# Linear attention beside a gated feed-forward block: Q projected token-wise next to K, denominators on VectorE, phi(q) turned by the DMA crossbar

## The chip, the cores and the metric

One core of one Trainium2 chip. The metric is device microseconds of one execution. Kernels sent together ran on the same chip, each beside runs of the kernel before. Traces count from the start of the span, which is 1.7 to 1.9 us shorter than the time of the same execution.

## The reference, cut to what matters

```python
xn = _layernorm(x)                               # x: 1 x 2048 x 576, bf16
q, k, v = split(xn @ wqkv)                       # 32 heads of 18
phi = lambda t: where(t > 0, t + 1, exp(t)) + 1e-6
kv  = einsum("bhsd,bhse->bhde", phi(k), v)
z   = einsum("bhsd->bhd", phi(k))
num = einsum("bhqd,bhde->bhqe", phi(q), kv)
den = einsum("bhqd,bhd->bhq", phi(q), z)[..., None] + 1e-6
A   = (num / den) @ wo
B   = (gelu(x_ @ w_gate) * (x_ @ w_up)) @ w_down # x_ = xn, 576 -> 4608 -> 576
out = x + A + B
```

The feed-forward block is most of the work. Attention has no softmax: it needs phi(k) for all tokens, then small 18x18 products per head, then one denominator per token and head.

## The kernel before: the parts that the change and the argument touch

The program runs a projection stage (16 tiles of 128 tokens), then four blocks of 512 tokens, each of them 18 gate/up steps and then a down projection. A number after "block", as in "block 3", means one such step of two units; "the second block" means the second 512 tokens. G is the product of xn and phi(k), summed over the tokens; with V's weights it gives kv. m is kv times wo, and the "m stage" builds it inside the first down projection. K comes out token-wise (tokens on partitions), Q channel-wise (channels on partitions), in five chunks of up to 126 channels; so phi(q) is at once in the layout that the final product wants.

```python
def k_half(n, hf):                               # token-wise: xnT is the stationary operand
    for kt in range(KT):
        nc.tensor.matmul(ps_all[:, k_bank(n, hf), :HALF], lhsT=xnT[:, kt, n*P:(n+1)*P],
                         rhs=wqkv_sb[:, kt, D + hf*HALF : D + (hf+1)*HALF], ...)

def q_unit(i):                                   # channel-wise: the weights are stationary
    for kt in range(KT):
        nc.tensor.matmul(ps, lhsT=wqkv_sb[:, kt, q0:q0+rows], rhs=xnT[:, kt, sc*SC:(sc+1)*SC], ...)

# phi before: relu and exp on ScalarE, (eps on GpSimd), max and add on VectorE

def den_mm(sc, c, bank):                         # denominators on TensorE, 512 tokens at once
    nc.tensor.matmul(ps, lhsT=zrep[:rows, c, :rows], rhs=pqT[:rows, c, sc*SC:(sc+1)*SC], ...)
    den_evac(sc, c, ps)                          # VectorE: PSUM -> SBUF, + eps

def den_norm(sc, c, q, pieces):
    for h in range(0, w, P):
        nc.vector.reciprocal(out=d[:, h:h+P], in_=d[:, h:h+P])
    # ... GpSimd then multiplies pqT by d

def gu_pair(sc, k):                              # one gate/up step
    for i in range(GUB):                         # GUB = 2 units, each on two PSUM banks
        if blk > 0:
            load_gu(blk + NWBUF - 1, i)          # weights three steps ahead, SyncE's queue
        u.p1()
    # ... load one slice of the down weights in steps 2 to 13 of the first block
    for i, (b, u) in enumerate(units):
        u.p2()
        nc.scalar.activation(out=gl[:], in_=ps_all[:, b[0], :], func=ACT.Gelu_apprx_tanh)
        nc.vector.tensor_tensor(out=hT[...], in0=ps_all[:, b[1], :], in1=gl[:], op=ALU.mult)

def m_stage(c, acc_bank):                        # inside the first down tile, every six matmuls
    for hf in range(2):
        b = (acc_bank + 2 + (2*c + hf) % 6) % 8
        nc.tensor.matmul(ps_all[:rows, b, :HALF], lhsT=kvT[...], rhs=wo2[...], ...)
```

## Time and profile before

| | before |
|---|---|
| time, median of the first 3 runs | 524.57 us |
| span of the trace | 521.7 us |
| TensorE busy | 99% |
| first projection matmul | 7.41 us |
| first gate/up starts, ends | 71.59, 142.93 us |
| period of the second and third block | 111.45, 111.46 us |

Read it as a chain of stages, each at TensorE's pace: the projection stage to 71.59 us, then four times gate/up (70.04 us of matmuls, 71.34 in the first block with the paired denominators) and down (40.2 us in the last block, 41.4 where denominator matmuls are hooked in). After the first 13 us TensorE hardly waits at all. So a change can help only by taking matmul time away, or by starting TensorE sooner. The prediction shows the lines behind this.

### The profile page before, as it was taken

What the parts mean: (1) busy time and instruction counts of PE and PEld (TensorE: products, weight loads), DVE (VectorE), ACT (ScalarE), POOL (GpSimd) and SP (SyncE); (2) the same over time, 40 slices, a digit from 0 to 9 for tenths busy, and PEclk for the clock granted to TensorE, in tenths of its full rate; (3) what the DMA queues carried; (4) which work ended last, traced back from release to release, by engine and by line L of the source; (5) the groups of instructions that cost most, each with busy time, mean ns of one, the idle gap of its engine ahead of it and who ended that gap; (6) DMA issues with size and microseconds to landing.
All of it is one profiled execution on the core that took longest, in us unless ns stands there. A gap on an engine that the chain in (4) does not pass through costs nothing.

```text
span 521.7 us, 10641 instructions
## 1 busy us (share of the span) xinstructions
PE 516.1 (99%) x4498; PEld 313.5 (60%) x4498; DVE 250.9 (48%) x436; ACT 143.1 (27%) x293; POOL 35.2 (7%) x55
## 2 busy tenths in 40 slices
PE   7999999999999999999999999999999999999997
PEld 6777755555587754444577744444777544445775
DVE  7996565876358323433388133333584233433101
ACT  6898442332320013323200032232000123322000
POOL 2021000211001100000012000000011000000000
PEclk9999999999999999999999999999999999999999
DMA  8334609899500045555300155555100355440000
GB/s 279 62 64 118 154 25 264 254 269 266 157 12 13 13 124 155 144 156 160 93 13 13 41 166 145 155 156 155 29 23 13 103 161 158 140 134 2 13 11 24
DMA packets 106282, 57.89 MB, mean 111 GB/s; under 512 B 13370, under 2 KB 105722, under 8 KB 106234
## 3 DMA queue, kind: packets, MB, share of 16 engines
q1 hardware_dynamic: 105626, 56.55, 38.8%
q8 instruction: 35, 0.57, 0.5%
q10 hardware_dynamic: 608, 0.66, 0.4%
q14 instruction: 13, 0.11, 0.1%
HBM read 52.86 MB, written 2.36 MB: 106 GB/s over the span
## 4 chain that ended last, share of the span: by engine, by line
PE 97%; DMA 1%; ACT 1%; DVE 0%; issue 0%
PE ps_all L313 55%; PE ps_all L677 27%; PE ps_all L289 4%; PE ps_all L682 4%; PE ps_all L245 3%; PE ps_all L342 3%; DMA wqkv_sb<-in_A_wqkv_dram 1%; PE ps_all L451 1%; PE ps_all L433 0%; PE ps_all L659 0%; ACT xnT L234 0%; ACT L114 0%; ACT phi_e L265 0%; ACT phi_e L269 0%; DVE hT L273 0%; DVE res L685 0%
## 5 line engine op out<-in xcount | busy, mean ns | idle before, releaser
L313 PE MATMUL ps_all<-xnT,wg 64*128 64x512 bf16 x1152 | 272.6, 376 | 0.0
L313 PE MATMUL ps_all<-xnT,wu 64*128 64x512 bf16 x1152 | 271.8, 376 | 0.0
L648 DVE TENSOR_TENSOR hT<-ps_all,gl 128x512 bf16<-128x512 f32 x144 | 99.5, 691 | 161.9 <-ACT gl L647 161.2
L647 ACT ACTIVATE gl<-ps_all 128x512 f32<-128x512 f32 x144 | 86.1, 598 | 314.3 <-PE ps_all L313 297.4
L313 PEld LDWEIGHTS <-wu 64*128 64x128 bf16 x1152 | 108.3, 94 | 66.3
L313 PEld LDWEIGHTS <-wg 64*128 64x128 bf16 x1152 | 108.3, 94 | 66.1
L677 PE MATMUL ps_all<-wd_sb,hT 128*128 128x288 bf16 x1152 | 147.0, 286 | 0.0
L677 PEld LDWEIGHTS <-hT 128*128 128x128 bf16 x1152 | 112.3, 98 | 30.6 <-issue 1.3
L475 DVE RECIPROCAL den_sb<-den_sb 126x128 f32<-126x128 f32 (+1 forms) x80 | 68.3, 911 | 0.5
L685 DVE TENSOR_TENSOR res<-ps_all,x_sb 128x288 bf16<-128x288 f32 x32 | 14.7, 458 | 88.0 <-PE ps_all L682 88.0
L313 PE MATMUL ps_all<-xnT,wr 64*128 64x512 bf16 x288 | 55.1, 376 | 0.0
L478 POOL TENSOR_TENSOR pqT<-pqT,den_sb 126x512 bf16<-126x512 bf16 (+3 forms) x25 | 24.2, 966 | 317.3 <-DVE den_sb L475 279.4
L682 PE MATMUL ps_all<-m_sb,pqT 126*128 126x288 bf16 (+1 forms) x160 | 24.9, 285 | 0.0
L313 PEld LDWEIGHTS <-wr 64*128 64x128 bf16 x288 | 14.4, 94 | 16.9 <-issue 0.7
L245 PE MATMUL ps_all<-wqkv_sb,xnT 128*128 128x288 bf16 x160 | 22.5, 286 | 0.9 <-DMA wqkv_sb<-in_A_wqkv_dram 0.8
L289 PE MATMUL ps_all<-hT,xn 128*128 128x288 bf16 (+4 forms) x176 | 22.4, 275 | 0.0
L289 PEld LDWEIGHTS <-xn 128*128 128x128 bf16 (+1 forms) x176 | 17.5, 102 | 4.1
L245 PEld LDWEIGHTS <-xnT 128*128 128x128 bf16 x160 | 15.4, 98 | 6.9 <-issue 1.4
L682 PEld LDWEIGHTS <-pqT 126*128 126x128 bf16 (+1 forms) x160 | 15.5, 97 | 4.1
L342 PE MATMUL ps_all<-xnT,wqkv_sb 128*126 128x512 bf16 (+1 forms) x70 | 17.4, 378 | 0.0
L273 DVE SCALAR_TENSOR_TENSOR hT<-ps_all,phi_e 128x288 bf16<-128x288 f32 x32 | 13.2, 450 | 4.6 <-ACT phi_e L269 4.0
L265 ACT ACTIVATE phi_e<-ps_all 128x288 f32<-128x288 f32 x32 | 12.9, 410 | 3.6 <-PE ps_all L245 2.1
(68 smaller groups left out, 173.8 us busy)
## 6 DMA issues: line engine op xcount, KB each, us to landing
wg<-in_B_w_gate_dram SPq DMA_DIRECT2D x72, 256.0 KB, 2.9
wu<-in_B_w_up_dram SPq DMA_DIRECT2D x72, 256.0 KB, 3.5
wd_sb<-in_B_w_down_dram SPq DMA_DIRECT2D x12, 432.0 KB, 4.6
wr<-in_B_w_gate_dram SPq DMA_DIRECT2D x72, 32.0 KB, 2.7
wr<-in_B_w_up_dram SPq DMA_DIRECT2D x72, 32.0 KB, 3.1
out_dram<-res SPq DMA_DIRECT2D x15, 144.0 KB, 1.8
x_sb<-in_A_x_dram SPq DMA_DIRECT2D x3, 576.0 KB, 7.1
wqkv_sb<-in_A_wqkv_dram SPq DMA_DIRECT2D x2, 576.0 KB, 4.7
```

The costliest lines, as they stand in the source:

```text
L245: nc.tensor.matmul(ps_all[:, k_bank(n, hf), :HALF], lhsT=xnT[:, kt, n * P:(n + 1) * P], rhs=wqkv_sb[:, kt, D + hf * HALF:D + (hf + 1) * HALF],
L273: nc.vector.scalar_tensor_tensor(out=out_, in0=ps, scalar=0.0, in1=e, op0=ALU.max, op1=ALU.add)
L289: nc.tensor.matmul(ps_all[:m, b, col:col + w], lhsT=xn[:, n, j0:j0 + m], rhs=pk[:, n, d0:d0 + w], start=(n == 0 and col == 0), stop=(n == ...
L313: return nc.tensor.matmul(self.outs[i], lhsT=self.lhs(i, rows, kt), rhs=self.rhs(i, rows, kt), start=start, stop=stop, skip_group_check=True,)
L342: nc.tensor.matmul(ps, lhsT=wqkv_sb[:, kt, q0:q0 + rows], rhs=xnT[:, kt, sc * SC:(sc + 1) * SC], start=(kt == 0), stop=(kt == KT - 1),)
L475: nc.vector.reciprocal(out=d[:, h:h + P], in_=d[:, h:h + P])
L478: nc.gpsimd.tensor_tensor(out=pqT[:rows, c, cols], in0=pqT[:rows, c, cols], in1=d, op=ALU.mult)
L647: nc.scalar.activation(out=gl[:], in_=ps_all[:, b[0], :], func=ACT.Gelu_apprx_tanh)
L648: nc.vector.tensor_tensor(out=hT[:, GUB * k + i, :], in0=ps_all[:, b[1], :], in1=gl[:], op=ALU.mult)
L677: nc.tensor.matmul(acc, lhsT=hT[:, f, j * P:(j + 1) * P], rhs=wd_sb[:, f, hs], start=(f == 0), stop=False,)
L682: nc.tensor.matmul(acc, lhsT=pqT[:rows, c, ts_], rhs=m_sb[:rows, c, hs], start=False, stop=(c == NCH - 1),)
L685: nc.vector.tensor_tensor(out=res[:, hs], in0=acc, in1=x_sb[:, n, hs], op=ALU.add)
```

## The change

Its intent: with a row of ones in the transposed tokens, the projection gives t + 1, so phi is max(min(exp(t), 1), t + 1): one exp and one VectorE pass. Q is projected like K, token by token. The denominators are then sums along the free axis, on VectorE, and TensorE does not have to do them; the scaled phi(q) has to be turned into the channel layout, by DMA crossbar transposes. The norm of tiles 3 to 15 goes to GpSimd. Cut to its core:

```diff
-    banks = _Ring([6, 7, 0, 1, 2, 3, 4, 5])
+    banks = _Ring([4, 5, 6, 7, 2, 3, 0, 1])
+    KQ_BANK = (6, 4)                                  # indexed by which: 0 is Q, 1 is K
+    def kq_mm(n, which, hf):                          # Q and K alike, 288 columns each
+        c = which * D + hf * HALF
+        for kt in range(KT):
+            nc.tensor.matmul(ps_all[:, KQ_BANK[which] + hf, :HALF], lhsT=xnT[:, kt, n*P:(n+1)*P],
+                             rhs=wqkv_sb[:, kt, c:c + HALF], ...)
+    def kq_exp(n, which, hf):
+        nc.scalar.activation(out=e[:], in_=ps_all[...], func=ACT.Exp, bias=neg1[:], scale=1.0)
+    def kq_phi(n, which, hf):
+        nc.vector.scalar_tensor_tensor(out=(pq, pk)[which][...], in0=e[:], scalar=1.0,
+                                       in1=ps_all[...], op0=ALU.min, op1=ALU.max)
 ... (q_unit, q_pair, q_relu, q_exp, q_eps, q_sum, den_mm, den_pair, den_evac, den_norm go)
     def ln_norm(n, c0=0, c1=D):
-        nc.vector.tensor_scalar(
+        (nc.vector if n < TD else nc.gpsimd).tensor_scalar(
 ...
+    def den_mul(n):    # VectorE: (pq + eps) * z, 576 columns
+    def den_inv(n):    # VectorE: reduce over 18, + eps, reciprocal of 32
+    def den_scale(n):  # VectorE: (pq + eps) * 1/den, two pieces
+    def den_transpose(n):
+        nc.sync.dma_start_transpose(pqT[:, :, n*P:(n+1)*P], den_pn[n][:])
 ... (a small planner now orders the projection stage from durations and landing times)
+    W_AT = {1: 5.60, 0: 7.90}                         # when K's and Q's weights are thought to land
+    den_jobs = [(job, n) for n in range(NS) for job in (den_mul, den_inv, den_scale, den_transpose)]
 ... in gu_pair, after each unit's eviction:
+            if den_jobs and blk > 0:
+                job, n = den_jobs.pop(0)
+                job(n)
```

K's weights are now asked for third on the one queue, ahead of the third x load, and Q's fifth; before, K's went on ScalarE's queue.

## The prediction

> **What bounds the kernel now.** I read the first page top down, then the chain of waits, then the chain in order of time, then the timeline at three places: the start, one projection period, the turn into the first down projection. The busy table and the chain come first.
>
> ```profile
> PE 516.1 (99%) x4498; PEld 313.5 (60%) x4498; DVE 250.9 (48%) x436; ACT 143.1 (27%) x293; POOL 35.2 (7%) x55
> ...
> PE 97%; DMA 1%; ACT 1%; DVE 0%; issue 0%
> PE ps_all L313 55%; PE ps_all L677 27%; PE ps_all L289 4%; PE ps_all L682 4%; PE ps_all L245 3%; PE ps_all L342 3%; DMA wqkv_sb<-in_A_wqkv_dram 1%; PE ps_all L451 1%; PE ps_all L433 0%; PE ps_all L659 0%; ACT xnT L234 0%; ACT L114 0%; ACT phi_e L265 0%; ACT phi_e L269 0%; DVE hT L273 0%; DVE res L685 0%
> ...
> L475 DVE RECIPROCAL den_sb<-den_sb 126x128 f32<-126x128 f32 (+1 forms) x80 | 68.3, 911 | 0.5
> ```
>
> 97% of the chain is TensorE, and gate/up (L313) and down (L677) are 82% of it; the change touches neither's own matmuls. The 68.3 us of reciprocals on VectorE never appear in the chain, so by themselves they are worth nothing. Busy TensorE is not TensorE at its limit, so I checked the spacing, in the chain in order of time (start, length, what):
>
> ```profile
> 65.78 77.21 PE ps_all L313 x714
> ...
> 185.48 70.04 PE ps_all L313 x648
> ...
> 260.86 4.41 PE ps_all L677 x36
> 266.11 4.41 PE ps_all L677 x36
> ...
> 508.70 4.41 PE ps_all L677 x36
> 513.73 4.41 PE ps_all L677 x36
> ```
>
> 648 half-array matmuls in 70.04 us are 108.1 ns each; those of the second token block, where there is nothing else, come gap-free. 714 x 108.1 = 77.2 us: the first block's line holds also the 54 of the paired Q units and 12 of the paired denominators, without a gap. In the down part the period is 513.73 - 508.70 = 5.03 us at the end and 266.11 - 260.86 = 5.25 where a denominator matmul is hooked in. So what is saved is matmul time that is removed, plus idle TensorE at the start. One projection period (timeline, TensorE):
>
> ```profile
> 26.79 0.91 PE L289 MATMUL ps_all<-hT,xn 128*128 128x288 bf16 x7
> 27.54 1.24 PE L342 MATMUL ps_all<-xnT,wqkv_sb 128*126 128x512 bf16 x5
> 28.62 1.39 PE L245 MATMUL ps_all<-wqkv_sb,xnT 128*128 128x288 bf16 x10
> 29.85 0.91 PE L289 MATMUL ps_all<-hT,xn 128*128 128x288 bf16 x7
> ```
>
> From start to start: seven G matmuls 0.75 us, five Q matmuls of 512 columns 1.08, ten K matmuls of 288 columns 1.23. The start, and the turn into the first down part:
>
> ```profile
> 7.41 0.77 PE L245 MATMUL ps_all<-wqkv_sb,xnT 128*128 128x288 bf16 x5 [0.79 <-DMA wqkv_sb<-in_A_wqkv_dram]
> ```
>
> ```profile
> 142.80 0.69 DVE L648 TENSOR_TENSOR hT<-ps_all,gl 128x512 bf16<-128x512 f32 x1 [2.33 <-ACT gl L647]
> ...
> 143.66 0.69 DVE L648 TENSOR_TENSOR hT<-ps_all,gl 128x512 bf16<-128x512 f32 x1 [0.17 <-ACT gl L647]
> ...
> 143.84 0.26 PEld L659 LDWEIGHTS <-kvT 126*126 126x126 bf16 x2
> ```
>
> The first K matmul starts at 7.41 because its weights land then; the copy of the transposed tokens had ended at 6.65 + 0.24 = 6.89, by the same view. At the turn, VectorE is done with the last gate/up bank at 144.35.
>
> **What the Trainium skill says.** "TensorE: Matmul & The Clock Gate", Back-to-back issue gap: a warm matmul of N columns costs N/2.4 + 2.5 ns. That is 215.8 for 512 and 122.5 for 288; the trace has 1.08/5 = 216 and 1.23/10 = 123. It agrees, and TensorE is warm. "VectorE: DVE Perf Modes", The TRN2 errata: an fp32 tensor_tensor takes (N+151)/0.96 ns; 512 gives 691, the trace's 691. I use it for the new VectorE passes. Its perf-mode tier table puts tensor_reduce at 1x, which no trace here shows yet. "GPSIMD Engine Reference", Engine selection: a one-input pass is roughly at line rate; the trace's 126x512 pass took 620 ns. "DMA: Bandwidth & Descriptors", Rules for kernel authors: a transpose next to ordinary DMAs needs no serializing. The before trace has its 12 transposes away from the heavy traffic (2.6 us to landing, 1.2 us of the issuing queue each), so it cannot confirm that.
>
> **The change part by part.**
>
> *Q projection.* Removed: 14 whole units x 5 x 0.216 = 15.1 us and 54 half-array matmuls x 0.108 = 5.8, together 20.9. Added: 16 tiles x 10 matmuls of 288 columns = 16 x 1.225 = 19.6. Saves 1.3 us.
>
> *Denominators off TensorE.* 12 half-array matmuls in the first gate/up: 12 x 0.108 = 1.3 us. 14 full ones hooked into the first three down parts: 14 x 0.216 = 3.0. Saves 4.3, all on the path.
>
> *Start.* K's weights go third on one queue, behind two x tiles (288 KB) in place of four. The windows table moved 171 GB/s in 0-5 us and 347 in 5-10, so 288 + 648 KB are through at about 5.2 us (estimate). The limit then is tile 0's transposition, and its last column block no longer waits for a GpSimd copy: about 6.8 where it was 7.41. One PE transposition fewer saves 0.3. Between 7.41 and 12.65 TensorE idled about 0.6 us; I keep 0.5.
>
> *A new wait after the last Q tile.* The third part of G now takes banks 4 and 5, the Q banks. Its first matmul needs exp (0.41) and phi (0.46) of the last Q half to be through, about 1.0 us after that half's last matmul. TensorE has 0.45 us of work meanwhile for the first bank and 0.1 for the second: idle 0.55 + 0.5 = 1.05 us. Before, Q and G never met there.
>
> *Sum of the projection stage.* 32 projections x 1.225 = 39.2, G 16 x 0.75 = 12.0, the rest of G 8.0, kv and z 1.75, transposes 0.6: 61.6. From 6.8, + 0.5 + 1.05: gate/up starts at 70.0, before at 65.78 + 54 x 0.108 = 71.6. Gain 1.6 us.
>
> *VectorE in that stage.* Per tile two stats 0.82, one aggregate 0.21, four phi 1.82: 2.85 us against a TensorE period of 2.45 + 0.75 = 3.2. The norm goes to GpSimd, 576/512 x 620 = 0.7 us (estimate). ScalarE: 0.49 + 4 x 0.41 = 2.1. All fit, VectorE with only 11% to spare.
>
> *VectorE in gate/up.* Gone: 68.3 (reciprocals) + 13.4 (evictions). New per tile, estimates by the page's formula: multiply 0.76, reduce 0.76 + small add and reciprocal 0.5, scale 0.68 + 0.23: 2.9 us over four units. With four eviction passes of 0.69 that is 5.7 of 4 x 1.945 = 7.8 us. It fits; nothing on the path.
>
> *The first down part.* The bank order became 4,5,6,7,2,3,0,1. The stage that builds m uses, six matmuls in, banks 0 and 1, which are now those of the last gate/up unit (before they were used at twelve). A den multiply (0.76) stands in VectorE's order between the last two evictions, so the last ends at 143.49 + 0.76 + 0.69 = 144.94 on the old clock, where that matmul was due at 143.96. Loss 1.0 us, once.
>
> *DMA.* 16 transposes of 160 KB in gate/up, eight of them in the first block, where the DMA engines are 86-107% busy from 80 to 130 us. Each costs about 0.9 us of the 16 engines (share 0.28 over 5 us with 1.6 transposes in 20-25 us). That delays loads by some 5 us at most by the end; gate weights are asked for three blocks (11.7 us) ahead and took up to 5.8 us to land. I expect no stall.
>
> Total: -1.6 - 1.3 - 3.0 + 1.0 = -4.9 us. 524.57 - 4.9 = 519.7.
>
> **The rivals.**
> 1. *VectorE becomes the bound of the projection stage.* For it: 89% load in a fixed order, with GpSimd beside it. Against: before, it was at 4.5-4.8 of 5 us busy in 15-40 us and TensorE never idled. If a tile took 3.4 in place of 3.2, it costs 3 us: 522.5 to 523.
> 2. *The transposes starve gate/up.* For: full DMA engines, and the queue that issues the weights now waits for VectorE's scale and then issues a transpose for 1.2 us. Against: the 11.7 us of lead, and that even the slowest weight load needed half of that. If it happened, 2 to 6 us in the first block: 522 to 526.
> 3. *The two bubbles are not there and the start is clean.* If VectorE and ScalarE are quicker than I order them, the whole 2 us stay: 517.5.
> 4. *Freeing VectorE and GpSimd speeds up gate/up.* Against: 108.1 ns a matmul is the issue gap itself. Nothing is to be had.
>
> **Range and chances.** Removed matmul time (5.6 us) is firm. The start is good to 1 us, each bubble to 1. That gives 517.0 to 522.4. Faster than 2% needs 10.5 us, twice what is removed, and no stall exists that could be added to it: 3%. Slower by 2% would take a stall of 15 us against the plan: 3%. Within 2%: 94%.
>
> **What would show it.** First real matmul at 6.8; a stage period of 3.2; gate/up from about 70.0; the first gate/up in 70.0 us and not 71.3; 5.03 us per half tile in all down parts after the first; about 1 us idle at the first G matmul on bank 4 and 5, released by VectorE's phi, and 1 us at the second m matmul pair, released by VectorE's hT. I am wrong if TensorE idles inside the projection stage on phi, or in gate/up on a weight DMA, or if gate/up's matmuls no longer come every 108 ns.

## The result, and the profile after

The changed kernel takes 519.90 us (median of 4, 519.53 to 520.3) beside 524.24 for the kernel before (4 runs). Ratio 0.9924, 95% interval 0.991 to 0.9938: 0.8% faster, inside 2%. A ratio here isn't quite the ratio of the medians (0.9917). So the gain is 4.0 us by the ratio and 4.3 by the medians, where 4.9 was predicted.

Stage by stage, from the traces (the end of the first gate/up is the start of the first matmul of the m stage):

| | before | changed | gain |
|---|---|---|---|
| first projection matmul | 7.41 | 7.11 | |
| first gate/up starts | 71.59 | 70.49 | 1.10 |
| length of first gate/up | 71.34 | 70.51 | 0.83 |
| from there to the second gate/up | 42.55 | 42.41 | 0.14 |
| second block | 111.45 | 110.37 | 1.08 |
| third block | 111.46 | 110.36 | 1.10 |
| fourth block to the end of the span | 113.31 | 113.66 | -0.35 |
| span | 521.7 | 517.8 | 3.9 |

The last row isn't TensorE's: from the fourth block's start to the start of the last group of matmuls are 109.6 us in both traces, and what follows that group takes 0.3 us longer in the changed one.

The page of the changed kernel, for the lines that answer to those of before:

```profile
PE 510.4 (99%) x4497; PEld 314.2 (61%) x4497; DVE 202.0 (39%) x407; ACT 133.5 (26%) x260; POOL 36.0 (7%) x32
...
PE 94%; DMA 3%; SPq 1%; ACT 1%; DVE 0%; POOL 0%; issue 0%
...
L213 POOL TENSOR_SCALAR xn<-x_sb,mv,rstd 128x576 bf16<-128x576 bf16 x13 | 29.6, 2287 | 8.7 <-ACT rstd L210 8.7
```

VectorE gave up 49 us of busy time, and the kernel gained 4. TensorE is still the chain, but 94% of it in place of 97%: DMA and its issuing queue (SPq) have come into it. The third line is one that the prediction had wrong by a factor of three: a norm on GpSimd takes 2287 ns.

The chain in order of time (start, length, what) says where those DMAs sit:

```profile
3.41 5.96 DMA wqkv_sb<-in_A_wqkv_dram
...
15.76 2.30 POOL xn L213
18.08 3.53 DMA xnT<-xn
...
23.80 2.45 PE ps_all L243 x20
26.25 0.74 PE ps_all L274 x7
...
60.20 8.74 PE ps_all L274 x71
...
127.66 5.42 DMA wr<-in_B_w_up_dram
133.13 7.09 PE ps_all L298 x63
...
183.41 70.04 PE ps_all L298 x648
```

There are three new waits: for Q's weights at the start, for the slow norm and transpose of an early tile, and for a small gate/up weight load near 133 us. The steady projection period is 2.45 + 0.74 = 3.20 us as planned (L243 is Q and K, L274 is G). And 71 G matmuls run in 8.74 us right after the last Q tile, without a gap: the bubble that I had predicted there isn't there. The two waits at TensorE, from its timeline, then the one at the turn into the first down projection:

```profile
7.11 1.39 PE L243 MATMUL ps_all<-wqkv_sb,xnT 128*128 128x288 bf16 x10
9.41 2.00 PE L243 MATMUL ps_all<-wqkv_sb,xnT 128*128 128x288 bf16 x15 [0.91 <-DMA wqkv_sb<-in_A_wqkv_dram]
```

```profile
141.48 0.75 DVE L358 SCALAR_TENSOR_TENSOR den_t<-pq,zb 128x576 f32<-128x576 bf16 x1
...
142.15 0.68 DVE L564 TENSOR_TENSOR hT<-ps_all,gl 128x512 bf16<-128x512 f32 x1
...
142.88 0.28 PE L574 MATMUL ps_all<-wo,kvT 126*126 126x288 bf16 x1 [0.56 <-DVE hT L564]
```

The den multiply stands between the last two evictions, and the second m matmul pair waits for the bank that the last eviction reads: it was due 0.12 us after 142.03 and came at 142.88, 0.73 us late.

### The profile page after: what moved, and what is told of

Same layout as the page of the kernel before. It is cut to its first block, busy times and chain, and to the rows that moved or that the text cites. A ratio compares the mean times of both kernels' runs of the same rounds, so it can differ in the third digit from the quotient of the medians. Undisturbed runs are those within 1.5% of the kernel's fastest.

```text
span 517.8 us, 10582 instructions
## 1 busy us (share of the span) xinstructions
PE 510.4 (99%) x4497; PEld 314.2 (61%) x4497; DVE 202.0 (39%) x407; ACT 133.5 (26%) x260; POOL 36.0 (7%) x32
## 4 chain that ended last, share of the span: by engine, by line
PE 94%; DMA 3%; SPq 1%; ACT 1%; DVE 0%; POOL 0%; issue 0%
PE ps_all L298 53%; PE ps_all L592 27%; PE ps_all L243 6%; PE ps_all L597 4%; PE ps_all L274 4%; DMA wqkv_sb<-in_A_wqkv_dram 1%; DMA wr<-in_B_w_up_dram 1%; DMA xnT<-xn 1%; POOL xn L213 0%; SPq L93 0%; PE ps_all L345 0%; DVE hT L564 0%; PE ps_all L574 0%; ACT phi_e L250 0%; DVE den_t L358 0%
## 5 line engine op out<-in xcount | busy, mean ns | idle before, releaser
L298 PE MATMUL ps_all<-xnT,wr 64*128 64x512 bf16 x288 | 56.2, 376 | 0.1
L243 PE MATMUL ps_all<-wqkv_sb,xnT 128*128 128x288 bf16 x320 | 42.5, 286 | 1.3 <-DMA wqkv_sb<-in_A_wqkv_dram 0.9
L243 PEld LDWEIGHTS <-xnT 128*128 128x128 bf16 x320 | 30.4, 98 | 9.0 <-issue 1.1
L250 ACT ACTIVATE phi_e<-ps_all,neg 128x288 f32<-128x288 f32 x64 | 31.6, 499 | 15.1 <-PE ps_all L243 11.4
L213 POOL TENSOR_SCALAR xn<-x_sb,mv,rstd 128x576 bf16<-128x576 bf16 x13 | 29.6, 2287 | 8.7 <-ACT rstd L210 8.7
L274 PE MATMUL ps_all<-hT,xn 128*128 128x288 bf16 (+4 forms) x176 | 22.6, 275 | 0.3 <-ACT xnT L232 0.3
L274 PEld LDWEIGHTS <-xn 128*128 128x128 bf16 (+1 forms) x176 | 17.6, 101 | 4.4 <-issue 0.5
L255 DVE SCALAR_TENSOR_TENSOR pq<-phi_e,ps_all 128x288 bf16<-128x288 f32 x32 | 14.5, 452 | 10.1 <-ACT phi_e L250 9.8
L255 DVE SCALAR_TENSOR_TENSOR hT<-phi_e,ps_all 128x288 bf16<-128x288 f32 x32 | 14.4, 453 | 3.4 <-ACT phi_e L250 3.0
L202 DVE BATCH_NORM_STATS2 stats<-x_sb 128x6 f32<-128x288 bf16 x32 | 13.0, 441 | 2.1 <-DMA x_sb<-in_A_x_dram 2.1
```

The costliest lines, as they stand in the source:

```text
L202: nc.vector.bn_stats(out=ln_raw[n][:, h, :], in_=x_sb[:, n, h * HALF:(h + 1) * HALF])
L213: (nc.vector if n < TD else nc.gpsimd).tensor_scalar(out=xn[:, n, c0:c1], in0=x_sb[:, n, c0:c1], scalar1=mv[:, n, 0:1], scalar2=rstd[:, n: ...
L243: nc.tensor.matmul(ps_all[:, KQ_BANK[which] + hf, :HALF], lhsT=xnT[:, kt, n * P:(n + 1) * P], rhs=wqkv_sb[:, kt, c:c + HALF], start=(kt == ...
L250: nc.scalar.activation(out=e[:], in_=ps_all[:, KQ_BANK[which] + hf, :HALF], func=ACT.Exp, bias=neg1[:], scale=1.0,)
L255: nc.vector.scalar_tensor_tensor(out=(pq, pk)[which][:, n, hf * HALF:(hf + 1) * HALF], in0=e_tiles[n, which, hf][:], scalar=1.0, in1=ps_al ...
L274: nc.tensor.matmul(ps_all[:m, b, col:col + w], lhsT=xn[:, n, j0:j0 + m], rhs=pk[:, n, d0:d0 + w], start=(n == 0 and col == 0), stop=(n == ...
```

## The experiments

My theory after this: the gain is the removed matmul time, about 5.6 us, and the rest of the account is waits at the edges. The rivals: VectorE's relief has a share in the gain; and each wait has another cause than the one that I name. Twelve kernels ran, on three chips, each beside the kernel before. The traces' main numbers first, side by side. The waits are the idle time that the profile gives, counted from the modelled end of the matmul before; from start to start they are about 0.17 us longer. "Late" is by how much the loads that block 13 issues (three steps ahead, so for block 16) were asked for after TensorE had begun block 13 (its start is gate/up's start + 13 x 3.891 us). Block 16, due at 132.75 us in the changed kernel, is where TensorE waited near 133.

| | time | ratio | wait for Q's weights | gate/up starts | first gate/up | late |
|---|---|---|---|---|---|---|
| changed | 519.90 | 0.9924 | 0.9 | 70.49 | 70.51 | 4.8 |
| changed again (control) | 520.50 | 0.9932 | 1.6 | 71.20 | 70.91 | 5.4 |
| Q on banks 4, 5 | 521.92 | 0.9965 | 1.6 | 72.34 | 70.98 | 5.3 |
| other ring | 519.67 | 0.9921 | 1.5, and 0.3 for K's | 71.53 | 70.95 | 5.3 |
| four tiles only | 519.96 | 0.9924 | 1.3 | 70.91 | 70.69 | 3.4 |
| plan's constants | 519.47 | 0.9916 | none | 70.19 | 70.48 | 5.0 |
| transposes from ScalarE | 521.22 | 0.9959 | 0.6 | 70.87 | 71.61 | 4.2 |
| all norms on VectorE | 518.91 | 0.9913 | 1.5 | 70.40 | 70.04 | 4.1 |
| paced down weights | 519.91 | 0.9920 | 1.0 | 70.89 | 70.03 | 2.8 |
| transposes behind loads | 520.10 | 0.9927 | 1.5 | 71.39 | 70.03 | 2.6 |
| combined | 518.01 | 0.9879 | none | 68.43 | 70.04 | 0.4 |

### What pays: VectorE time or TensorE time? (b_norecip, b_den128)

Both are the kernel before with one thing less; both give a wrong result.

```diff
-        for h in range(0, w, P):
-            nc.vector.reciprocal(out=d[:, h:h + P], in_=d[:, h:h + P])
```

> The kernel before with its 80 reciprocals on VectorE left out (68.3 us of VectorE's time; the result is wrong on purpose). Theory: VectorE's denominator work lay beside TensorE's and was worth nothing; the time stays at 524.2, within 0.3 us, and TensorE's placement does not move. Rival: the reciprocals held evictions and so TensorE, and freeing VectorE is part of what the change gained: 1 us or more less.

Measured: 523.37 us beside 523.65, ratio 1.0003 (0.999 to 1.0015). 68 us less VectorE work moved nothing. The theory holds.

```diff
-        nc.tensor.matmul(ps, ..., rhs=pqT[:rows, c, sc * SC:(sc + 1) * SC], ...)
+        nc.tensor.matmul(ps[:, 0:P], ..., rhs=pqT[:rows, c, sc * SC:sc * SC + P], ...)
```

> The kernel before with the 14 denominator matmuls of 512 columns in the down projections cut to 128 columns (the result is wrong on purpose; VectorE's and GpSimd's work stay as they are). Theory: removed TensorE time is paid in full: 14 x (216 - 56) ns = 2.2 us less, 522.0. Rival: a matmul hooked in this way costs its wait or its eviction and not its columns; then the time stays near 524.2.

Measured: 521.59 us, ratio 0.9966 (0.9953 to 0.9978), 0.34% of 523.65 or 1.8 us less. The chain in order of time of the run without reciprocals, then of the run with short denominator matmuls:

```profile
185.40 70.03 PE ps_all L313 x648
296.86 70.04 PE ps_all L313 x648
```

```profile
185.00 70.04 PE ps_all L313 x648
295.66 70.04 PE ps_all L313 x648
```

The period from one gate/up to the next is 111.46 in the first and 110.66 in the second: 0.80 us for five matmuls shortened by 160 ns each. The denominator matmuls are paid one for one, and the reciprocals' VectorE time not at all.

### The bubble after the last Q tile (a_qbanks)

```diff
-    KQ_BANK = (6, 4)
+    KQ_BANK = (4, 6)
```

> The changed kernel with Q's and K's PSUM banks exchanged, so that the third part of G does start on the banks that the last Q tile leaves. My theory is that the 1.05 us bubble that I predicted after the last Q tile is real physics, and was missing only because I had read the bank table the wrong way round (Q is on 6 and 7, K on 4 and 5). It expects TensorE to idle about 1.0 us at the first two G matmuls after the last Q tile, released by phi on VectorE, and the time to rise by 1.0 us over the changed kernel's 519.9, to 520.9. The rival, that exp and phi are quick enough to be hidden by themselves, expects no idle there and 519.9.

Timeline of TensorE in this run:

```profile
59.55 1.39 PE L243 MATMUL ps_all<-wqkv_sb,xnT 128*128 128x288 bf16 x10
61.40 0.28 PE L274 MATMUL ps_all<-hT,xn 128*128 128x288 bf16 x1 [0.47 <-DVE pq L255]
62.01 8.78 PE L274 MATMUL ps_all<-hT,xn 128*128 128x289 bf16 x70 [0.33 <-DVE pq L255]
```

Ten projection matmuls take 1.22 us, so the first G matmul was due at 60.77 and came 0.63 us late; the second was due 0.12 us after the first and came 0.49 us late. (The brackets count from the modelled end of the matmul before, and so show less.) The bubble is real when the banks meet: 1.12 us, released by phi of Q, where I had said 0.55 + 0.5. From the start of these ten to gate/up are 12.79 us here and 11.67 in the changed kernel, the same 1.12. So the mechanism and its size were right and the premise wrong: I had taken the bank table to be (K, Q) where it is indexed (Q, K). The time rose from 0.9924 to 0.9965, 0.41% or 2.1 us, more than the bubble; the trace also has 0.7 us more wait for Q's weights than the changed kernel's first one, and 0.5 us more in the first gate/up. Together these are 2.3 us, which is the difference of the two spans (520.1 and 517.8). The last two vary from run to run, as the control shows.

### The same kernel again (a_same)

No edit.

> The changed kernel once more, not altered, as the control of this call. In the traces so far the same code waited 0.6 to 1.8 us for the Q weights at the start and 0.8 to 3 us on a weight DMA in the first gate/up block. Theory: these two waits are of the DMA engines' timing and vary from execution to execution, so this trace shows 0.6 to 1.8 us for the first and 0.3 to 2 for the second, and the time is 0.9924 of before within 0.0013. Rival: they are fixed by the code, and this trace repeats 0.91 and 0.8.

Measured: 520.50 us (519.58 to 521.38), ratio 0.9932 (0.9919 to 0.9945). The wait for Q's weights was 1.6 us where it had been 0.91, and the first gate/up 70.91 us where it had been 70.51. The code is the same. Both waits are on DMA, and both vary by more than most of the effects looked for below. So small edits are judged by the piece of the trace that they touch, and times only where the intervals allow it. What makes the landing vary isn't known from these runs.

### The wait at the turn into down (a_ring, a_den4)

```diff
-    banks = _Ring([4, 5, 6, 7, 2, 3, 0, 1])
+    banks = _Ring([4, 5, 6, 7, 0, 1, 2, 3])
```

> The changed kernel with the PSUM ring in the order 4,5,6,7,0,1,2,3, so that the last gate/up unit of a block leaves banks 2 and 3, which the stage that builds m asks for twelve matmuls into the first down projection in place of six. Theory: the 0.73 us that TensorE lost in that stage waiting for VectorE's last eviction was the bank order's doing; it goes, and the time falls by 0.7 us to about 519.2. Rival: VectorE's den multiply in front of the eviction holds the matmul whatever the bank, and the idle time stays or moves to another matmul: 519.9.

Timeline of this run at the turn:

```profile
142.97 0.75 DVE L358 SCALAR_TENSOR_TENSOR den_t<-pq,zb 128x576 f32<-128x576 bf16 x1
143.52 0.41 PE L574 MATMUL ps_all<-wo,kvT 126*126 126x288 bf16 x2
143.63 0.68 DVE L564 TENSOR_TENSOR hT<-ps_all,gl 128x512 bf16<-128x512 f32 x1
```

The two matmuls of the second pair run as one group while the last eviction is only beginning, with the den multiply still in its place: with this bank order there is no wait. From the end of the first gate/up to the second are 41.68 us in place of 42.41, so the 0.73 us is gained in full there. The time, 0.9921, shows no gain over 0.9924; this trace waited 1.8 us for the projection weights (1.5 of it for Q's) and its first gate/up took 70.95 us. On time the run is inconclusive; on the mechanism it isn't.

```diff
-            if den_jobs and blk > 0:
+            if den_jobs and blk > 0 and (sc > 0 or den_jobs[0][1] < TPC):
```

> The changed kernel with the denominator jobs of only the four tiles that the first down projection needs done in the first gate/up block (four crossbar transposes there in place of eight, none while the down weights stream in the second half), the others later. Theory: the transposes are what delays the gate/up weights; the wait of about 0.5 us on the small weight DMA near 133 us goes, the first gate/up block takes 70.05 us from first to last matmul, and with no den multiply before the last eviction the 0.73 us wait of the m stage goes too: 1.2 us less, 518.7. Rival: the weights are late because of the down weights alone; then only the 0.7 us go and the wait on the weight DMA stays: 519.2.

Measured: 519.96 us, ratio 0.9924, no gain: a miss. With no den multiply between the last evictions the second m pair came 0.33 us late (143.08, due at 142.75) in place of 0.73: the ring alone costs a third of a microsecond, the den multiply the rest. The weight wait did not go. It moved from 133 to 118 us, and the first gate/up took 70.69 us. So the loads can run late with four transposes, all in the first half (one trace); neither my theory (it goes) nor the rival (it stays at 133, with the down weights alone to blame) describes that.

### What delays the gate/up weights? (a_actq, a_pace, a_defer)

The issuing queue of the changed kernel, around block 3, which TensorE begins at 70.49 + 3 x 3.89 = 82.2 us:

```profile
80.65 0.59 SPq L530 DMA_DIRECT2D wd_sb<-in_B_w_down_dram  x1
83.64 1.24 SPq L385 DMA_TRANSPOSE pqT<-pn  x1
85.39 0.39 SPq L162 DMA_DIRECT2D wg<-in_B_w_gate_dram  x1
```

The queue stands from 81.2 to 83.6 us, until VectorE has scaled the tile; then it issues the transpose; then the load that block 3 issues for block 6, 3.2 us late. I had written that this lead was 11.7 us and safe.

```diff
-        nc.sync.dma_start_transpose(pqT[...], den_pn[n][:])
+        nc.scalar.dma_start_transpose(pqT[...], den_pn[n][:])
```

> The changed kernel with the 16 crossbar transposes of phi(q) issued from ScalarE's queue in place of the queue that issues the weights. It tells two ways apart in which the transposes could delay the gate/up weights. If it is the issuing queue (1.2 us of issue for each transpose, and the wait for VectorE's scale in front of it), the wait of about 0.5 us on the weight DMA near 133 us goes, and the time falls by 0.5 us or, if ScalarE's evictions are now held by the issue, rises by up to 1 us with idle in gate/up on PSUM. If it is the DMA engines' bandwidth, the wait on the weight DMA stays: 519.9.

Measured: 521.22 us, ratio 0.9959. SyncE's queue was relieved (43.7 us of issue in the first gate/up in place of 58.2), and yet the first gate/up grew to 71.61 us: 1.6 us over its 70.04. The small weight loads took up to 7.0 us to land (median 5.6) in place of 6.3 (4.3). ScalarE was held as well: before the gelu at 135.72 us it stood for 5.2 us, a transpose's issue among them, and the second m pair came 1.21 us late in place of 0.73. In gate/up itself TensorE's waits are on a small weight load (0.2 and 0.8 us). So the run mixes the ways that it was to tell apart, and the time rose by more than the 1 us that I had allowed. It does show that relieving this queue isn't enough: with the transposes on a second queue the weights land later. Why is open. The DMA engines' share was 1.12 to 1.22 from 80 us on, but 0.98 to 1.32 in the changed kernel, so it doesn't tell the two apart; and in the second block these transposes took 4.9 us to land (median) in place of 2.6.

```diff
-        elif sc == 0 and k >= 2:
+        elif sc == 0 and k >= 2 and k % 4 != 1:
             load_wd_slice()
```

> The changed kernel with the twelve slices of down weights spread over blocks 2 to 16 in place of 2 to 13 (every fourth block asks for none); nothing else moves. Theory: in 80 to 130 us the DMA engines are asked for 576 + 432 KB of weights and 80 KB of transposes per 3.89 us block, more than they move (259 to 287 GB/s), so the loads fall behind; at 576 + 324 + 80 KB they keep up, the wait on the weight DMA near 133 us goes, and the first gate/up block takes 70.1 us in place of 70.5: 0.5 us less. Rival: the lateness comes from the transpose's place in the issuing queue and stays.

```diff
+        while turned:                              # after the step's weight loads
+            den_transpose(turned.pop(0))
-    ... for job in (den_mul, den_inv, den_scale, den_transpose)]
+    ... for job in (den_mul, den_inv, den_scale, turned.append)]
```

> The changed kernel with each crossbar transpose moved behind the next block's weight loads in the issuing queue, so that the loads no longer stand behind a wait for VectorE's scale. Theory of the order: block 3's weights were asked for at 85.39, 3.2 us after TensorE had begun that block, and that lateness is the lead that is missing near 133; with it restored to under 1 us at block 3 the wait on the weight DMA goes, 0.5 us less. Rival, the engines' bandwidth: the loads are asked for earlier but land no earlier, and a wait of about 0.5 us or more stays.

The chain in order of time of the run with paced down weights, then of the run with transposes behind the loads:

```profile
70.95 69.19 PE ps_all L298 x640
```

```profile
71.45 69.19 PE ps_all L298 x640
```

Both took the wait away altogether: 640 matmuls in one piece, where the changed kernel's chain breaks near 133 us; the first gate/up is 70.03 us in each, and no weight DMA is left among TensorE's waits. I had set them up as rivals and they aren't. The loads run out of lead, and relief at either place is enough. That they start late behind a transpose is shown by the queue; that the engines are asked for more than they move is not shown, since pacing also takes issues out of the same queue, and a block's 1088 KB (of 1024 bytes) in 3.89 us would be 286 GB/s (estimate), where the windows table has 223 to 287 GB/s moved between 80 and 130 us. Each result rests on one trace. The "late" column goes with it: at 4.1 us late or less with the transposes on SyncE's queue TensorE didn't wait, at 4.8 or more it did, the four-tile run excepted, whose wait fell in an earlier block. In time neither is clear of the control: 0.9920 (0.9908 to 0.9932) and 0.9927 (0.9915 to 0.9938) against 0.9932.

### The order at the start (a_plan)

```diff
-    W_AT = {1: 5.60, 0: 7.90}
+    W_AT = {1: 6.80, 0: 9.40}
-            step(("norm", n), "POOL", 0.80, ...
+            step(("norm", n), "POOL", 2.29, ...
-                step(("exp", n, which, h), "ACT", 0.45, ...
+                step(("exp", n, which, h), "ACT", 0.50, ...
```

> The changed kernel with three constants of its ordering plan set to what its own trace shows: Q's weights land at 9.4 us (planned 7.9), a GpSimd norm takes 2.29 us (planned 0.80), an exp 0.50 (planned 0.45). Only the order of the instructions changes. Theory: TensorE's 0.91 us wait for the Q weights and the waits of 0.3 us for the late tiles come from a plan that puts Q of tile 0 too early; with K of tile 1 ahead of it the waits shrink, and gate/up starts 0.5 to 1.0 us before 70.5: 518.9 to 519.4. Rival: the start is bound by what lands when, not by the order, and as much idle turns up elsewhere: 519.9.

Measured: 519.47 us, ratio 0.9916 (0.9903 to 0.993), not clear of 0.9924. Gate/up started at 70.19 us, 0.3 sooner. Timeline of TensorE:

```profile
10.09 0.77 PE L243 MATMUL ps_all<-wqkv_sb,xnT 128*128 128x288 bf16 x5 [1.50 <-DVE hT L255]
```

The wait for the weights is gone, and in its place K of tile 1 waits 1.5 us for phi of tile 0 (hT in the line: phi(k) lies in that buffer at this stage), which still holds K's bank. The rival (the idle time turns up elsewhere) is nearer than the theory, and it says what to do: give K of tile 1 another bank.

### Is VectorE the bound of the projection stage? (a_alldve)

```diff
+ND = 16
-        (nc.vector if n < TD else nc.gpsimd).tensor_scalar(
+        (nc.vector if n < ND else nc.gpsimd).tensor_scalar(
```

> The changed kernel with all 16 norms on VectorE, none on GpSimd (the plan knows it). VectorE then has 2.85 + 0.43 = 3.28 us of work per tile against TensorE's period of 3.20. Theory: VectorE becomes the bound of the projection stage by a little: 16 x 0.08 = 1.3 us at most, less what the quick norms gain at the start (tile 3's norm took 2.29 us on GpSimd and its transpose was waited for, 0.3 to 0.6 us): 519.9 to 521.0, with TensorE waiting for phi. Rival: the slow GpSimd norm is the larger harm, and the time falls by up to 0.6 us.

Measured: 518.91 us (518.83 to 519.4), ratio 0.9913 (0.9899 to 0.9926). No wait on phi came, so the theory was wrong and the rival nearer. Less the wait for Q's weights, gate/up starts at 68.9 us, 0.7 sooner than in the changed kernel and in the control (69.6 in both), and the weight wait of 0.5 us in the first gate/up is gone. As a time it isn't clear of 0.9924 or of the control's 0.9932. The windows table of this run (columns: busy us of TensorE, of its weight load, of VectorE, ScalarE, GpSimd):

```profile
30.00:40.00 10.00, 10.00 (x86) 8.04 (x84) 8.84 (x26) 6.83 (x18) 0.00 (x0) 1.00 0.25 49
```

TensorE is busy in all of the 10 us with VectorE at 8.84, and no tile's transpose is waited for over 0.2 us. The timeline of VectorE shows why there was no deficit:

```profile
31.24 0.45 DVE L256 SCALAR_TENSOR_TENSOR pq<-phi_e,ps_all 128x288 bf16<-128x288 f32 x1 [0.33 <-ACT phi_e L251]
...
31.85 0.45 DVE L256 SCALAR_TENSOR_TENSOR pq<-phi_e,ps_all 128x288 bf16<-128x288 f32 x1
32.22 0.45 DVE L203 BATCH_NORM_STATS2 stats<-x_sb 128x6 f32<-128x288 bf16 x1
...
34.48 0.46 DVE L256 SCALAR_TENSOR_TENSOR pq<-phi_e,ps_all 128x288 bf16<-128x288 f32 x1 [0.38 <-ACT phi_e L251]
```

In each tile's 3.2 us VectorE still waits 0.3 to 0.4 us for ScalarE's exp. My 3.28 us added up the lengths of instructions that overlap (a pass of 0.45 us, and the next begins 0.37 after it); the eight of a tile fit in about 2.85. The first gate/up also lost its weight wait here (late 4.1); I have no cause for that.

### All together (a_best)

All norms on VectorE, the other ring, paced down weights, transposes behind the loads (the edits above), the plan's landing times and exp, and, new, K of tile 1 on Q's banks and Q of tile 0 on K's:

```diff
+    def kq_bank(n, which, hf):
+        return {(0, 0): 4, (1, 1): 6}.get((n, which), KQ_BANK[which]) + hf
```

> A version meant to beat both: the changed kernel with all norms on VectorE, the PSUM ring 4,5,6,7,0,1,2,3, down weights spread over blocks 2 to 16, transposes behind the next block's loads, and at the start K of tile 1 on Q's banks ahead of Q of tile 0, which then takes K's banks (so TensorE has 1.2 us of work while Q's weights land). Theory: it keeps the 5.6 us of removed matmul time and loses the waits: about 0.8 us at the start, 0.3 for late tiles, 0.5 on the weight DMA, 0.7 before the second m matmul pair; gate/up starts at 69.5 or earlier, and the time is 2.0 us below the control's, about 517.7, ratio 0.988 to before. Rival: part of these waits only moves; then 518.5 to 519.5.

Measured: 518.01 us (516.21 to 518.21, 4 runs), ratio 0.9879 (0.9862 to 0.9896), with correct results; 2.5 us below the control's median and clear of it. TensorE's timeline at the start, then the chain in order of time:

```profile
7.10 2.61 PE L247 MATMUL ps_all<-wqkv_sb,xnT 128*128 128x288 bf16 x20
```

```profile
68.50 70.04 PE ps_all L302 x648
...
180.15 70.04 PE ps_all L302 x648
```

From the first projection matmul at 7.10 to gate/up at 68.43 us are 61.3 us, the sum of the matmuls that the prediction made (61.6), so hardly any gap is left there. The run changes all of this at once, so it doesn't say what each part is worth. The traced execution was the fastest of the four, 516.21 us; the others took 1.6 to 2.0 us longer and have no trace, so what they waited for is open.

## Why the prediction was right

The time was 519.9 us where 519.7 was predicted, but that closeness is in part luck. Two errors of about 1 us nearly balance in the start of gate/up (a bubble that wasn't there, and idle time that wasn't foreseen). And the prediction counted from 524.57 us, where the kernel before measured 524.24 beside the changed one: of the 4.9 us of gain that it forecast, 4.0 to 4.3 came. Step by step:

- **Removed matmul time.** Right. The Q projection's period is 3.20 us; the second and third block are 1.08 and 1.10 us shorter, five denominator matmuls of 216 ns each. The two runs on the kernel before show it for the denominators: their matmuls are paid in full and the reciprocals not. For the Q projection's 1.3 us only the sums and the traces speak; no run takes it alone.
- **"Gate/up starts at 70.0".** It started at 70.49. Of the terms, the first matmul came at 7.11 in place of 6.8: tile 0's copies were through at 6.40, but seven dummy matmuls and tile 1's transposition stood before it on TensorE. The bubble "after the last Q tile" (1.05 us) was not there, through my misreading of the bank table, and is 1.12 us when it is. In its place TensorE idled 1.8 us at the start (63.4 us from the first matmul to gate/up, less 61.6 of matmuls) where I had kept 0.5: waiting for Q's weights, which I had forgotten to follow although I had worked out K's, and for the tiles behind GpSimd.
- **"576/512 x 620 = 0.7 us" for a norm on GpSimd.** Mis-sized: 2.29 us. The row that I scaled was a pass with two immediate scalars and f32 data; the norm has two per-partition operands and bf16. Which of these makes it slow no run separates. It fits in the 3.2 us period, and cost only the early tiles.
- **"4 x 0.41" for ScalarE.** Mis-sized without effect: an exp with a per-partition bias took 499 ns. The Trainium skill says so ("ScalarE: Activation LUTs", What ACT_TABLE_LOAD costs: a [128,1] operand adds about 93 ns); 0.41 was the relu's row, which has none. The trace agrees: 499 - 410 = 89 ns.
- **The first gate/up in 70.0 us, "I expect no stall".** Wrong by 0.5 us (0.9 in the control). The failed step is "gate weights are asked for three blocks (11.7 us) ahead": behind the transposes they were asked for up to 5.4 us late, and landing took up to 6.5. My second rival described it, but its 2 to 6 us were too much.
- **"Loss 1.0 us, once" in the m stage.** Right in place and releaser, 0.73 us in size, because consecutive VectorE instructions overlap a little (the den multiply is 0.75 us long, and the eviction begins 0.67 after it), and because the matmul that waits is the second of its pair, due 0.12 us later than the one I took. The run with the other ring removes it.
- **VectorE in gate/up.** Right: the five passes of a tile took 0.75 + 0.74 + 0.18 + 0.35 + 0.67 + 0.23 = 2.92 us (the scale is two of the six instructions), 2.9 predicted, and off the path.
- **Rival 1, VectorE as the bound.** It didn't happen, and not even with all norms on it. The 2.85 us per tile added up lengths that overlap, so VectorE had more to spare than the 11% that I gave it.

The chances held: removing 5.6 us of 524 can't reach 2%.

## What to carry to other kernels

Where one engine is busy 99% of the span, price a change in that engine's own instructions and then look only at the edges: the first weights, the hand-over of a buffer between stages, the queue that issues the loads. Look for a DMA that waits for a compute engine and stands in a queue ahead of loads that someone needs; here, putting it behind them took TensorE's wait away in the trace, though the gain was too small to be clear in the time. Repeat the unchanged kernel before judging an edit of half a microsecond: here the same program's DMA waits at the start alone ranged over 0.7 us.

## What the Trainium skill lacked or had wrong

- "TensorE: Matmul & The Clock Gate", Back-to-back issue gap: the prediction read the formula N/2.4 + 2.5 ns as what a matmul costs in a stream. The page gives it for an isolated matmul and puts a sustained stream of 512 columns at about 131 ns each. Here five of them without a gap took 1.08 us, 216 ns each: the formula's figure, and not the page's sustained one.
- "GPSIMD Engine Reference", Engine selection, has one-input passes at roughly line rate. A 128x576 bf16 tensor_scalar with two per-partition operands took 2287 ns on GpSimd, 424 on VectorE; 126x512 f32 with immediate scalars took 620. The page doesn't tell the forms apart.
- "DMA: Bandwidth & Descriptors", Rules for kernel authors, says that a transpose next to ordinary DMAs needs nothing. The results were correct in every run that wasn't wrong on purpose, so for correctness this agrees. For time the page has sequencer cycles and a bandwidth of other transposes, but not these: one 128x640 transpose held the issuing queue for 1.2 us (2.7 at worst), and in the first gate/up, with the DMA engines busy, it took 5.2 us to land (median) in place of 2.6 in the second.
- No page gives how much DMA landing varies in one program. The same kernel waited 0.9 and 1.6 us for the same weights in two traces.
- "VectorE: DVE Perf Modes", The TRN2 errata: (N+151)/0.96 fitted the new passes (748 and 743 ns at 576 columns, formula 757, the second a tensor_reduce at 1x as the perf-mode tier table has it). It doesn't hold for reciprocal: 353 ns at 32 columns and 911 at 128, or 5.8 ns a column, for which the page gives no figure.
